# Attention in steps of twenty rows, spread over the four quarters of TensorE

## The chip, the cores and the metric

The kernel runs on one NeuronCore of a Trainium2 chip. The metric is the device time of one execution in microseconds (us). Three runs of the kernel before took 1311.48, 1315.52 and 1314.14 us, with a median of 1314.14 us.

## The reference

The program is three stages in a row. All inputs and the result are 32-bit floats.

```python
# attention: batch 4, 12 heads, 448 rows, head size 64
scores = scale * (q @ k.T)                        # for each head
scores = einsum('bhij,hg->bgij', scores, w_pre)   # premix: the 12 heads are mixed
attn = softmax(scores)                            # along j
attn = einsum('bhij,hg->bgij', attn, w_post)      # postmix: mixed again
x = attn @ v                                      # 1792 rows x 768
x = elu(x @ w_in) @ w_out                         # 768 -> 2048 -> 768
# then each row goes through the one of 8 experts that its gate picks
out[rows of e] = gate * (relu(x @ w1[e]) @ w2[e]) # 768 -> 1024 -> 768
```

The change lies in the first stage alone.

## The kernel before, in words

The first stage (function attention, lines 145 to 424) works through 4 batches of 448 rows in 16 chunks of 110 or 118 rows (CHUNKS, line 26), and through each chunk in 11 or 12 groups of ten rows (a few of nine; GRP, line 27). There are 180 groups in all.

For each chunk, q times k (qk, line 224) is worked out for two heads at a time: the two heads lie in the two halves of 64 partitions, and each takes half of TensorE's rows. q and k are split into a high and a low part in the format fp32r (split_k, split_k_lo, split_q, split_q_lo), and three products (line 233) make up one 32-bit product. The scores leave PSUM by ScalarE and VectorE (qk_out, lines 241 and 243) into a tile st that has rows of the chunk in its partitions and heads beside each other.

The mix over heads needs the heads in the partitions. So for each group one DMA (relayout, line 248), issued on SyncE's queue (SP), moves ten rows of st times 12 heads into 120 partitions of a tile sp. Premix (line 254) is then one 32-bit product of 120x120 weights (a block of w_pre for each of the ten rows) with 448 columns. VectorE takes the maximum (rowmax, line 260), ScalarE the exponential with its sum (expo, line 268), VectorE inverts the sums (norm, lines 277 and 278) and scales the weights of the second mix by them (scale, lines 287 and 289). Postmix (line 298) has the exponentials as its loaded operand and the scaled weights as its moving one, so that it transposes on the way: four 32-bit products with 120 columns. ScalarE copies the result into mt (mt_out, line 305), which has keys in its partitions. Times v (av, line 322) runs for each chunk with two heads in two halves of TensorE's columns, and av_out (lines 329 and 330) sends the result to DRAM.

A 32-bit matmul of the program stands in the trace as two pairs of LDWEIGHTS (weight load) and MATMUL, each of which streams its columns twice; an fp32r one is one pair that streams them once.

The order of the work on every engine is written out by hand: each piece is filed under a slot and an order number (the calls of at, lines 368 to 424), all pieces are sorted by these two numbers, and each engine then does its instructions strictly in that order. Slot x has premix of group x (order 10), postmix of group x-4 (11), then q times k (12) and times v (13) where they fall due. Waits are set by the tiles: a piece waits for the tiles that it reads, and for a free buffer. Around these pieces lies the decoding of some weights of the second stage (lines 128 to 133), 48 halves of it.

The second and third stage (moe1, moe2) begin when the attention is done, with line 523 as the first product.

Of the kernel before, what the change touches and what calls it, by code (L numbers as in the profile page):

```python
# [5 lines left out]
F32 = mybir.dt.float32  # L6
# [13 lines left out]
JC, NJ = 112, 4  # L20
# [5 lines left out]
CHUNKS = [110, 110, 110, 118]  # L26
GRP = [[10] * 11, [10] * 11, [10] * 11, [10] * 10 + [9, 9]]
# [12 lines left out]

def token_orders():


    orders = []
    for n, gs in zip(CHUNKS, GRP):
        G = len(gs)
        starts = [sum(gs[:g]) for g in range(G)]
        order = [0] * n
        for g, T in enumerate(gs):
            for i in range(T):  # L50
                order[g + G * i] = starts[g] + i
        orders.append((order, starts))
    return orders
# [85 lines left out]
for _c in range(NCH):  # L139
    S0.append(S0[-1] + len(GRP[_c % 4]))  # L140
NSLOT = S0[-1]
LAG = 4


def attention(tc, pools, at, q, k, v, kron_pre, kron_post, dec_jobs, xscr):

# [8 lines left out]
    kpre = sb.tile([120, 120], F32, name="kpre")  # L155
    nc.gpsimd.dma_start(kpre, kron_pre)
    nc.vector.tensor_scalar(kpre, kpre, -1.0 / 8.0, None, ALU.mult)
    kpo = sb.tile([120, 120], F32, name="kpo")
    nc.gpsimd.dma_start(kpo, kron_post)
    dec = Decoder(nc, early, 2, 4)  # L160

    (kraw, kr, qraw, qs, qp, st, sp, pre, mxs, pt, sms, rec, kpt, pst, mt, vt, avp,
     draw, dsteps) = ({} for _ in range(19))


    def keys(b, u):
        kr[b, u] = early.tile([128, 2, S], F32R, name="kr", tag="kr", bufs=6)

    def values(b):
        vt[b] = sb.tile([JC, NJ, H, D], F32, name="vt", tag="vt", bufs=2)  # L170
# [6 lines left out]
    def scores(cc):  # L177
        st[cc] = early.tile([118, H, S], F32, name="st", tag=f"st{cc % 2}")

    def load_k(b, u):  # L180
        if b == 0:

            if u == 0:
                scores(0)
                kraw[0] = early.tile([128, H, S], F32, name="k0", tag="st1")
            t = kraw[0][:, u, :]
        else:
            t = early.tile([128, S], F32, name="kraw", tag="kraw", bufs=4)
        nc.sync.dma_start(t, k[b, :, u, :])
        kraw[b, u] = t  # L190

    def split_k(b, u):
        if b:
            keys(b, u)
        if b == 0:
            nc.scalar.activation(kr[b, u][:, 0], kraw[b, u], AF.Copy)
        else:
            nc.vector.tensor_copy(kr[b, u][:, 0], kraw[b, u])

    def split_k_lo(b, u):  # L200
        t = kr[b, u]
        nc.vector.tensor_tensor(t[:, 1], kraw.pop((b, u)), t[:, 0].bitcast(F32), ALU.subtract)

    def load_q(cc, u):
        b, c = divmod(cc, 4)
        n, o = CHUNKS[c], sum(CHUNKS[:c])
        t = early.tile([128, 3 * 118], F32, name="qraw", tag="qraw", bufs=2)
        nc.sync.dma_start(t[:, :3 * n], q[b, :, 6 * o + 3 * n * u:6 * o + 3 * n * (u + 1)])
        qraw[cc, u] = t

    def split_q(cc, u):
        n = CHUNKS[cc % 4]
        t = qs[cc, u] = early.tile([128, 2, 3 * 118], F32R, name="qs", tag="qs", bufs=3)
        nc.scalar.activation(t[:, 0, :3 * n], qraw[cc, u][:, :3 * n], AF.Copy)

    def split_q_lo(cc, u):
        n = CHUNKS[cc % 4]
        t = qs[cc, u]
        nc.vector.tensor_tensor(t[:, 1, :3 * n], qraw.pop((cc, u))[:, :3 * n], t[:, 0, :3 * n].bitcast(F32), ALU.subtract)

    def bank(nm, tag):
        return (ps_qk if tag == "qk" else ps).tile([128, 512], F32, name=nm, tag=tag, bufs=4 if tag == "qk" else 2)

    def qk(cc, u):

        n = CHUNKS[cc % 4]
        tag = {2: "pre", 3: "post"}.get(u, "qk") if cc == 0 else "qk"
        p = qp[cc, u] = [bank("p_qk", tag) for _ in range(2)]
        kk, qq, c = kr[cc // 4, u], qs[cc, u // 3], slice(u % 3 * n, (u % 3 + 1) * n)
        for i, (x, y) in enumerate(((0, 0), (0, 1), (1, 0))):  # L230
            for e in range(2):
                r = slice(64 * e, 64 * e + 64)
                mm(p[e][:n, :S], lhsT=qq[r, x, c], rhs=kk[r, y, :], start=(i == 0), stop=(i == 2))  # L233

    def qk_out(cc, h):
        n = CHUNKS[cc % 4]
        if h == 0 and cc:
            scores(cc)
        src = qp[cc, h // 2][h % 2][:n, :S]
        if h % 2 if cc == 0 else h % 4 == 1:  # L240
            nc.vector.tensor_copy(st[cc][:n, h, :], src)
        else:
            nc.scalar.activation(st[cc][:n, h, :], src, AF.Copy)  # L243

    def relayout(cc, g):
        G, T = len(GRP[cc % 4]), GRP[cc % 4][g]
        t = sb.tile([120, S], F32, name="sp", tag="sp", bufs=4)
        nc.sync.dma_start(t[:12 * T], st[cc][g:g + G * (T - 1) + 1:G])
        sp[cc, g] = t

    def premix(cc, g):
        R = 12 * GRP[cc % 4][g]
        p = bank("p_pre", "pre")
        mm(p[:R, :S], lhsT=kpre[:R, :R], rhs=sp.pop((cc, g))[:R], start=True, stop=True)  # L254
        pre[cc, g] = p
# [1003 lines left out]
```

## Time and profile before

| | |
|---|---|
| median of three runs | 1314.14 us |
| the profiled execution's own time | 1312.17 us |
| its span, first to last instruction | 1310.3 us |
| mean granted clock of TensorE over the span | 0.984 |
| attention, until the first product of the second stage | 479.6 us |
| TensorE busy over the span | 1257.4 us (96%) |
| VectorE / ScalarE / GpSimd busy | 834.2 / 749.9 / 46.0 us |

A busy time is the time in which at least one instruction of the engine was under way. The page gives it for the whole span, and the view of windows for any stretch. The granted clock is the share of TensorE's clock that was let through (1.00 is 2.4 GHz, 0.50 is 1.2 GHz). The chain that ended last is read backwards from the last instruction, at each step to what released it. In the timeline, the time from the start of one entry to the start of the next on the same engine tells what an instruction really costs there, since instructions overlap at their ends.

### The profile page before, as it was taken

How to read it: one execution, taken by the hardware profiler on the slowest of the kernel's cores; microseconds unless marked ns; L12 is line 12 of the kernel's file. 1: busy time of each engine (PE TensorE's matmuls, PEld its weight loads, DVE VectorE, ACT ScalarE, POOL GpSimd, SP SyncE). 2: the span in 40 equal slices, each digit the busy share in tenths (PEclk: the TensorE clock that was granted, in tenths of full speed). 3: DMA queues.
4: the chain of work that ended last, by engine and by line, in shares of the span. 5: the costliest groups of instructions: out<-in, count | busy, mean ns of one | idle time of the engine just before them, and what ended most of it. 6: DMA issues, size and time to landing. Idle time of an engine off the chain costs nothing.

```text
span 1310.3 us, 23113 instructions
## 1 busy us (share of the span) xinstructions
PE 1257.4 (96%) x8622; PEld 1095.4 (84%) x8622; DVE 834.2 (64%) x1815; ACT 749.9 (57%) x1521; POOL 46.0 (4%) x60
## 2 busy tenths in 40 slices
PE   5899999999999989999999999999997999999996
PEld 3577777777677778998899899989996999999996
DVE  4678778778877647887545654664445555666663
ACT  5677767767677555566555555655534444455552
POOL 0000000000000000000000000000001011111110
PEclk8999999999999999999999999999996999999998
DMA  5668667666866448320010011001007647566661
GB/s 153 183 192 243 188 183 234 200 187 200 233 184 180 137 136 331 126 83 2 22 57 8 1 33 46 8 1 43 1 3 250 206 157 231 166 225 222 228 217 56
DMA packets 107340, 181.97 MB, mean 139 GB/s; under 512 B 24755, under 2 KB 75411, under 8 KB 107220
## 3 DMA queue, kind: packets, MB, share of 16 engines
q1 hardware_dynamic: 104468, 168.29, 41.2%
q0 software_dynamic: 2752, 12.12, 2.8%
q8 instruction: 70, 1.15, 0.4%
q14 instruction: 50, 0.41, 0.1%
HBM read 115.88 MB, written 26.95 MB: 109 GB/s over the span
## 4 chain that ended last, share of the span: by engine, by line
PE 90%; DMA 4%; ACT 2%; DVE 2%; issue 1%; SPq 0%; POOL 0%; POOLq 0%; DVEq 0%; ACTq 0%
PE p_h L523 17%; PE acc L585 16%; PE p_h L1031 11%; PE p_pre L254 10%; PE p_post L298 10%; PE p_z L1016 8%; PE p_av L322 6%; PE p_qk L233 5%; PE p_y L1031 3%; DMA sp<-st 2%; PE tp L78 1%; PE p_t L78 1%; DMA xraw<-xscr 1%; DMA raw<-in_w_out_dram 0%; DMA kpre<-in_kron_pre_dram 0%
## 5 line engine op out<-in xcount | busy, mean ns | idle before, releaser
L298 PEld LDWEIGHTS p_post<-kp,pt 120*112 120x112 f32 (+1 forms) x1440 | 175.6, 179 | 74.2 <-issue 50.7
L254 PE MATMUL p_pre<-sp,kpre 120*120 120x448 f32 x360 | 173.2, 564 | 17.2 <-DMA sp<-st 10.8
L298 PE MATMUL p_post<-kp,pt 120*112 120x120 f32 (+1 forms) x1440 | 178.7, 268 | 4.1 <-DVE kp L289 3.7
L260 DVE TENSOR_REDUCE mx<-p_pre 120x1 f32<-120x448 f32 x180 | 111.8, 621 | 75.6 <-PE p_pre L254 74.8
L305 ACT ACTIVATE mt<-p_post 112x480 f32<-112x480 f32 x180 | 103.7, 576 | 77.0 <-PE p_post L298 72.8
L585 PE MATMUL acc<-gh,woh 128*128 128x448 f32 x384 | 142.4, 371 | 0.2 <-ACT gh L482 0.2
L523 PE MATMUL p_h<-xh,wih 128*128 128x448 f32 x384 | 142.3, 371 | 0.0
L585 PE MATMUL acc<-gl,woh 128*128 128x448 f32 x384 | 140.6, 366 | 1.6 <-DVE gl L483 1.6
L523 PE MATMUL p_h<-xh,wil 128*128 128x448 f32 x384 | 140.7, 366 | 0.1
L523 PE MATMUL p_h<-xl,wih 128*128 128x448 f32 x384 | 140.5, 366 | 0.0
L585 PE MATMUL acc<-gh,wol 128*128 128x448 f32 x384 | 140.4, 366 | 0.0
L541 DVE SCALAR_TENSOR_TENSOR th<-rm,th 128x448 f32<-128x448 f32 x64 | 40.0, 625 | 138.2 <-ACT rm L534 138.2
L268 ACT ACTIVATE pt<-p_pre,mx 120x448 f32<-120x448 f32 x180 | 113.3, 630 | 2.3 <-DVE mx L260 2.1
L243 ACT ACTIVATE st<-p_qk 110x448 f32<-110x448 f32 (+1 forms) x141 | 71.7, 542 | 67.0 <-PE p_qk L233 64.2
L1031 PE MATMUL p_h<-xgl,w1h 128*128 128x256 f32 (+1 forms) x384 | 109.7, 286 | 0.2 <-DVE xgl L995 0.2
L1031 PE MATMUL p_h<-xgh,w1h 128*128 128x256 f32 (+1 forms) x384 | 109.9, 286 | 0.0
L1031 PE MATMUL p_h<-xgh,w1l 128*128 128x256 f32 (+1 forms) x384 | 109.6, 285 | 0.0
L100 DVE TENSOR_TENSOR w2l<-w2raw,w2h 128x768 fp32r<-128x768 f32 (+1 forms) x60 | 60.7, 1011 | 51.8 <-ACT w2h L98 51.8
L482 ACT ACTIVATE gh<-g 128x448 fp32r<-128x448 f32 x64 | 37.0, 579 | 93.6 <-DVE g L542 93.6
L322 PEld LDWEIGHTS p_av<-mt,vt 112*64 112x64 f32 x1536 | 73.9, 137 | 17.1 <-ACT st L243 16.4
L531 ACT ACTIVATE rm<-p_h 128x448 f32<-128x448 f32 x64 | 34.7, 542 | 88.2 <-PE p_h L523 88.2
L322 PE MATMUL p_av<-mt,vt 112*64 112x110 f32 (+1 forms) x1536 | 83.5, 262 | 0.8
(159 smaller groups left out, 2547.4 us busy)
## 6 DMA issues: line engine op xcount, KB each, us to landing
sp<-st SPq DMA_DIRECT2D x172, 210.0 KB
w1raw<-in_w_dram SPq DMA_DIRECT2D x64, 384.0 KB
w2raw<-in_w_dram SPq DMA_DIRECT2D x48, 384.0 KB
raw<-in_w_in_dram SPq DMA_DIRECT2D x32, 384.0 KB
raw<-in_w_out_dram SPq DMA_DIRECT2D x32, 384.0 KB
wscr<-wdec SPq DMA_DIRECT2D x32, 192.0 KB
win<-wscr SPq DMA_DIRECT2D x16, 384.0 KB
w2raw<-in_w_dram SPq DMA_DIRECT2D x12, 512.0 KB
```

The source lines that it names most:

```text
L233: mm(p[e][:n, :S], lhsT=qq[r, x, c], rhs=kk[r, y, :], start=(i == 0), stop=(i == 2))
L243: nc.scalar.activation(st[cc][:n, h, :], src, AF.Copy)
L254: mm(p[:R, :S], lhsT=kpre[:R, :R], rhs=sp.pop((cc, g))[:R], start=True, stop=True)
L260: nc.vector.tensor_reduce(mx[:R], pre[cc, g][:R, :S], AX.X, ALU.min)
L268: nc.scalar.activation(e[:R], pre.pop((cc, g))[:R, :S], AF.Exp, bias=mxs.pop((cc, g))[:R], scale=-1.0, accum_out=sms[cc, g // 2][:R, g % 2 ...
L298: mm(p[:JC, j * R:j * R + R], lhsT=e[:R, j * JC:(j + 1) * JC], rhs=kp[:R, :R], start=True, stop=True)
L305: nc.scalar.activation(mt[cc][:, :, :, off:off + T], pst.pop((cc, g)), AF.Copy)
L322: mm(p[64 * e:64 * e + 64, u % 2, :n], lhsT=vt[cc // 4][:, j, 2 * u + e, :], rhs=mt[cc][:, j, 2 * u + e, :n], start=(j == 0), stop=(j == N ...
L523: mm(p[:, :S], lhsT=a[:, c], rhs=m, start=(i == 0), stop=(i == 17))
L585: mm(acc[d][:, :S], lhsT=a[:, c], rhs=m, start=(f == 0 and i == 0), stop=(f == NF - 1 and i == 2))
L1016: mm(zp[p][j, a][:, :384], lhsT=h2[h][:, i, c], rhs=w[:, a * 384:(a + 1) * 384], start=(i == 0 and m == 0), stop=(i == NFE - 1 and m == 2))
L1031: mm(q[:, :N], lhsT=a[:, kk, :], rhs=m[:, kk, :], start=(j == 0), stop=(j == len(seq) - 1))
```

## The change

Chunks have 120, 120, 120 and 88 rows, and each is worked through in units of 20 rows (the last unit of the fourth chunk has 8). There are 92 units: 88 of 20 rows and four of 8.

A unit's rows are dealt to the four quarters of TensorE, 64 rows by 64 columns each. Five rows times 12 heads make 60 partitions, so that a quarter mixes five rows.

- **q times k** takes q and k as they are, in 32 bits, without a split: for two heads four matmuls of 64x64 weights with 448 columns, one in each quarter. The splits of q and k, and their loads into separate tiles, go.
- **The moves** into sp are four DMAs for a unit instead of one for a group: each moves 5 rows times 12 heads (60 partitions of 1792 bytes). They are issued by GpSimd.
- **Premix** is four matmuls of 60x64 weights with 448 columns, one in each quarter, into two PSUM banks.
- **rowmax and expo** run on 128 partitions, two of each for a unit. The inverted sums and the scaled weights of a unit are made by three VectorE instructions.
- **Postmix** is 32 matmuls of 60x64 weights with 60 columns, eight in each quarter, into one PSUM tile of two banks with a single buffer. One ScalarE instruction of 960 elements copies it out.
- **Times v** has the keys in blocks of 128, 128, 128 and 64 (the rest of the last block is zeros) and 120 or 88 columns.
- **The order** is filed by half slots: q times k (order 9) and premix (10) in the first half of a slot, times v (9) and postmix of the unit two before (10) in the second; where q times k falls into a second half it stands there. Three PSUM banks are for premix, two for postmix, two for q times k and one for times v.

```diff
-CHUNKS = [110, 110, 110, 118]
-GRP = [[10] * 11, [10] * 11, [10] * 11, [10] * 10 + [9, 9]]
+CHUNKS = [120, 120, 120, 88]
+UNITS = [[(5, 2)] * 6] * 3 + [[(5, 2)] * 4 + [(4, 1)]]
...
-        for i, (x, y) in enumerate(((0, 0), (0, 1), (1, 0))):
+        for a in range(2):
             for e in range(2):
-                mm(p[e][:n, :S], lhsT=qq[r, x, c], rhs=kk[r, y, :], start=(i == 0), stop=(i == 2))
+                r, c = slice(64 * e, 64 * e + 64), u % 3 * 128 + 64 * a
+                mm(p[64 * a:64 * a + 64, e, :S], lhsT=qq[r, c:c + 64], rhs=kk[r], start=True, stop=True)
...
-        t = sb.tile([120, S], F32, name="sp", tag="sp", bufs=4)
-        nc.sync.dma_start(t[:12 * T], st[cc][g:g + G * (T - 1) + 1:G])
+        t = sp[cc, g] = sb.tile([128, 2, S], F32, name="sp", tag="sp", bufs=3)
+        for r in range(nr):
+            for c in range(2):
+                f, d = first_row(g, r, c, nr), STEP[cc % 4]
+                nc.gpsimd.dma_start(t[64 * r:64 * r + 12 * T, c], st[cc][f:f + d * (T - 1) + 1:d])
...
-        mm(p[:R, :S], lhsT=kpre[:R, :R], rhs=sp.pop((cc, g))[:R], start=True, stop=True)
+        ban = pre[cc, g] = [ps.tile([128, 512], F32, name="p_pre", tag="pre", bufs=3) for _ in range(nr)]
+        for c in range(2):
+            for r in range(nr):
+                x = slice(64 * r, 64 * r + 12 * T)
+                mm(ban[r][64 * c:64 * c + 64, :S], lhsT=kpre[x], rhs=t[x, c, :], start=True, stop=True)
...
-        for j in range(NJ):
-            mm(p[:JC, j * R:j * R + R], lhsT=e[:R, j * JC:(j + 1) * JC], rhs=kp[:R, :R], start=True, stop=True)
+        for j in range(4):
+            for r in range(nr):
+                for s in range(2 * j, 2 * j + 2):
+                    k0 = min(s, 6)
+                    for c in range(2):
+                        x = slice(64 * c, 64 * c + 12 * T)
+                        mm(p[64 * (s % 2):64 * (s % 2) + 64, 2 * c + r, j * 12 * T:(j + 1) * 12 * T],
+                           lhsT=e[x, r, 64 * k0:64 * k0 + 64],
+                           rhs=kp[x, r].rearrange("p (h i) -> p h i", i=5)[:, :, :T], start=True, stop=True)
...
-            at(x - (3 if g or cc else 2), 1, relayout, cc, g)
+            at(x - 2, 1, relayout, cc, g)
             at(x, 10, premix, cc, g)
-            at(x + LAG, 11, postmix, cc, g)
-            at(x + LAG + 1, 28, mt_out, cc, g)
+            at(x + LAG + .5, 10, postmix, cc, g)
+            at(x + LAG + 1, 26, mt_out, cc, g)
```

The number of decoded halves stays 48, and the second and third stage are as they were.

## Rows read from the trace of the kernel before

**Rows 1.** The page: busy time of each engine over the span with its share and instructions, then busy tenths in 40 equal slices of the span, with the granted clock and the share of the DMA engines.

```profile
PE 1257.4 (96%) x8622; PEld 1095.4 (84%) x8622; DVE 834.2 (64%) x1815; ACT 749.9 (57%) x1521; POOL 46.0 (4%) x60
...
PE   5899999999999989999999999999997999999996
...
PEclk8999999999999999999999999999996999999998
```

**Rows 2.** Busy time by window: stretch, its length, then busy time (and instructions) of each engine, granted clock, DMA share, GB/s.

```profile
core 0: us, PE busy (x) PEld busy (x) DVE busy (x) ACT busy (x) POOL busy (x), PEclk, DMA share, GB/s
...
18.64:468.76 450.12, 437.08 (x3738) 327.89 (x3738) 335.09 (x944) 308.61 (x744) 0.00 (x0) 0.99 0.66 195
468.76:479.60 10.84, 6.71 (x43) 5.70 (x44) 8.12 (x18) 8.31 (x17) 0.00 (x0) 0.90 0.67 230
200.00:250.00 50.00, 49.38 (x425) 37.25 (x424) 40.52 (x114) 35.37 (x85) 0.00 (x0) 1.00 0.80 235
479.60:1310.30 830.70, 806.33 (x4806) 756.61 (x4805) 482.69 (x837) 424.57 (x745) 44.47 (x54) 0.98 0.32 107
```

**Rows 3.** The chain that ended last: start, us, what, in the first 20 us, at one chunk boundary, and at the end of attention.

```profile
7.09 6.58 PE p_qk L233 x34
...
14.38 4.12 DMA sp<-st
18.64 1.82 PE p_pre L254 x2
...
105.43 6.13 DMA sp<-st
...
477.80 1.80 PE p_post L298 x8
479.60 7.98 PE p_h L523 x36
```

**Rows 4.** Timeline of TensorE: start, us, what, with counts, at 250 us (chunks of 110 rows) and at 150 us (times v with 118 rows).

```profile
250.42 0.92 PE L254 MATMUL p_pre<-sp,kpre 120*120 120x448 f32 x2
251.18 0.95 PE L298 MATMUL p_post<-kp,pt 108*112 108x108 f32 x8
...
253.60 1.47 PE L233 MATMUL p_qk<-kr,qs 64*110 64x448 f32 x12
255.10 1.73 PE L322 MATMUL p_av<-mt,vt 112*64 112x110 f32 x32
256.75 1.01 PE L254 MATMUL p_pre<-sp,kpre 120*120 120x448 f32 x2
257.60 0.98 PE L298 MATMUL p_post<-kp,pt 120*112 120x120 f32 x8
258.42 0.92 PE L254 MATMUL p_pre<-sp,kpre 120*120 120x448 f32 x2
...
151.96 1.83 PE L322 MATMUL p_av<-mt,vt 112*64 112x118 f32 x32
153.72 1.01 PE L254 MATMUL p_pre<-sp,kpre 120*120 120x448 f32 x2
```

**Rows 5.** Timeline of TensorE at 611 us, in the second stage, where line 649 runs six 32-bit matmuls with 448 columns in four column strips of 32: first within 0.03 us, then until the next group.

```profile
611.53 0.58 PE L649 MATMUL lg<-x,wg 128*32 128x448 f32 x4
...
611.53 1.70 PE L649 MATMUL lg<-x,wg 128*32 128x448 f32 x12
613.16 0.47 PE L585 MATMUL acc<-gh,woh 128*128 128x448 f32 x1
```

**Rows 6.** Timeline of ScalarE at 208 us, and one row at 254 us.

```profile
208.42 0.58 ACT L305 ACTIVATE mt<-p_post 112x480 f32<-112x480 f32 x1
208.88 0.64 ACT L268 ACTIVATE pt<-p_pre,mx 120x448 f32<-120x448 f32 x1
209.39 0.22 ACT L268 ACTIVATION_READ_ACCUMULATOR pt<-p_pre,mx 120x1 f32 x1
209.48 0.63 ACT L129 ACTIVATE dec_p<-dec_p,ebias 128x384 uint32<-128x384 uint32 x1
...
255.10 0.98 ACT L243 ACTIVATE st<-p_qk 110x448 f32<-110x448 f32 x2
```

**Rows 7.** Timeline of VectorE from 208.3 to 212.3 us.

```profile
208.81 0.35 DVE L128 TENSOR_SCALAR dec_p<-raw 128x384 uint32<-128x384 uint32 x1
209.08 0.36 DVE L130 TENSOR_SCALAR dec_m<-raw 128x384 uint32<-128x384 uint32 x1
209.35 0.28 DVE L287 TENSOR_SCALAR kp<-kpo,sm 120x120 f32<-120x120 f32 x1
209.88 0.63 DVE L260 TENSOR_REDUCE mx<-p_pre 120x1 f32<-120x448 f32 x1 [0.25 <-PE p_pre L254]
210.42 0.38 DVE L329 COPY xc<-p_av 128x220 f32<-128x220 f32 x1
210.72 0.49 DVE L219 TENSOR_TENSOR qs<-qraw,qs 128x330 fp32r<-128x330 f32 x1
211.13 0.55 DVE L131 SCALAR_TENSOR_TENSOR dec_m<-raw,dec_m 128x384 f32<-128x384 uint32 x1
211.59 0.16 DVE L277 TENSOR_SCALAR sm<-sm 120x2 f32<-120x2 f32 x1
211.79 0.17 DVE L278 RECIPROCAL sm<-sm 120x2 f32<-120x2 f32 x1
211.99 0.28 DVE L287 TENSOR_SCALAR kp<-kpo,sm 120x120 f32<-120x120 f32 x1
212.19 0.62 DVE L260 TENSOR_REDUCE mx<-p_pre 120x1 f32<-120x448 f32 x1
```

**Rows 8.** Groups of instructions on GpSimd: line, engine, operation, count, busy us and mean ns of one, idle time before.

```profile
L1067 POOL DMA_INDIRECT out_dram<-yrow,put x18 | 24.6, 1368 | 252.4 <-ACT w1h L98 116.2 <-DVE yrow L1058 70.8 <-DVE yrow L1065 64.0
L978 POOL DMA_INDIRECT xg<-x2rows,tok x18 | 18.6, 1033 | 1002.5 <-DMA x2rows<-row 991.4 <-DVE xgl L995 6.2 <-issue 3.7
...
L156 POOL DMA_DIRECT2D kpre<-in_kron_pre_dram x1 | 0.7, 726 | 0.9 <-POOLq L1249 0.9
L159 POOL DMA_DIRECT2D kpo<-in_kron_post_dram x1 | 0.6, 577 | 0.0
```

**Rows 9.** Line 248 by itself: the issue of a move on SP (shortest, median, longest, ns), and who waited for the moves in the whole span (us, times).

```profile
L248 SPq DMA_DIRECT2D sp<-st x180: 760/808/2208, 14.4 to 463.2; - x180
...
  PE p_pre L254: 10.8, 7
```

More of the change, by code (lines that the diff above doesn't have):

```diff
@@ L38, in blocks, with first_row @@
     return [min(128, n - o) for o in range(0, n, 128)]
+def first_row(g, r, c, nr):
+    return 64 * r + 2 * g + c if nr == 2 else 64 * c + 2 * g
 def token_orders():
     orders = []
[L45 to L52, printed above, removed]
+    for us, d in zip(UNITS, STEP):
+        order = [-1] * 128
+        for g, (T, nr) in enumerate(us):
+            for r in range(nr):
+                for c in range(2):
+                    for i in range(T):
+                        order[first_row(g, r, c, nr) + d * i] = 20 * g + (c * nr + r) * T + i
+        orders.append(order)
     return orders
@@ L177, in scores @@
     def scores(cc):
-        st[cc] = early.tile([118, H, S], F32, name="st", tag=f"st{cc % 2}")
+        st[cc] = early.tile([128, H, S], F32, name="st", tag=f"st{cc % 2}")
     def load_k(b, u):
[L181 to L189, printed above, removed]
@@ L190, in load_k @@
-        kraw[b, u] = t
-    def split_k(b, u):
         if b:
             keys(b, u)
[L195 to L202, printed above, removed]
+        elif u == 0:
+            scores(0)
+        nc.sync.dma_start(ks[b, u], k[b, :, u, :])
     def load_q(cc, u):
@@ L345, in attention, with half, take @@
     use = {}
-    def take(slot, **cost):
+    def half(y, order, fn, *args):
+        at(y / 2, order, fn, *args)
+    def take(y, **cost):
         for e, c in cost.items():
-            use[e, slot] = use.get((e, slot), 0) + c
-        return slot
+            use[e, y] = use.get((e, y), 0) + c
+        return y
     def room(lo, hi, **cost):
-        return take(min(range(lo, max(lo, hi) + 1), key=lambda x: max(use.get((e, x), 0) + c for e, c in cost.items())), **cost)
-    def block(cc, u):
+        return take(min(range(lo, max(lo, hi) + 1), key=lambda y: max(use.get((e, y), 0) + c for e, c in cost.items())), **cost)
@@ L368, in attention @@
     for cc in range(NCH):
-        z, G = S0[cc], len(GRP[cc % 4])
+        z = S0[cc]
         for u in range(6):
-            x = block(cc, u)
-            at(x, 12, qk, cc, u)
-            at(x, 33, qk_out, cc, 2 * u)
-            at(x if cc else x + 1, 33 if cc else 29, qk_out, cc, 2 * u + 1)
-            if u % 2 and cc:
-                take(x, act=162 - 300, dve=54 - 300)
-        for g in range(G):
+            y = when(cc, u)
+            half(y, 9, qk, cc, u)
+            half(y + 1, 5, qk_out, cc, u)
+            take(y + 1, act=54 if u % 2 else 90, dve=62 if u % 2 else 0)
@@ L390, in attention @@
-            take(x + 3, dve=20)
-            at(x + LAG, 11, postmix, cc, g)
-            at(x + LAG + 1, 28, mt_out, cc, g)
-            take(x + LAG + 1, act=57)
+            at(x + LAG, 20, scale, cc, g)
+            for r in range(nr):
+                at(x, 22, rowmax, cc, g, r)
+                at(x + 1, 24, expo, cc, g, r)
+            at(x + LAG + .5, 10, postmix, cc, g)
+            at(x + LAG + 1, 26, mt_out, cc, g)
+            take(2 * x, dve=185, act=200)
+            take(2 * x + 1, act=60)
@@ L414, in attention @@
-            at(f - 6 if cc else (-20, -18)[u], 3, load_q, cc, u)
-            at(x, 40, split_q, cc, u)
-            at(room(x + 1, f - 1, dve=50) if cc else x, 41, split_q_lo, cc, u)
+            half(when(cc, 3 * u) - 8 if cc else (-40, -36)[u], 3, load_q, cc, u)
     N = 2 * len(dec_jobs)
```

289 lines of the change are left out of this document (129 added, 160 removed).

## The prediction, made before the changed kernel was built

> **What bounds the kernel now.** I read the page first. TensorE is busy 96% of the span and no other engine over 64% [rows 1], so the question is what the change does to TensorE's time, and who is next when that falls. The granted clock stands at 9 (full) in nearly every slice, so no stage is waiting for clock.
>
> The windows come next, since the change touches one stage only. From the first premix at 18.64 us to the last at 468.76 us TensorE is busy 437.1 of 450.1 us, VectorE 335.1 and ScalarE 308.6; 13 us of the stretch are waits. The stage ends at 479.6 us, and the 830.7 us behind it are untouched [rows 2]. The chain of waits confirms it: short DMA pieces at the start (4.12 us of a move before the first premix) and at a chunk boundary (6.13 us), else TensorE's own products [rows 3]. So attention is bound by TensorE's columns, with 18.6 us of lead-in and 10.8 us of tail.
>
> What each product costs is read from the timeline, from start to start [rows 4]. Premix: 251.18 - 250.42 = 0.76 us. Postmix: 258.42 - 257.60 = 0.82 us. Q times k for four heads (12 pairs of weight load and matmul): 255.10 - 253.60 = 1.50 us. Times v for four heads (32 pairs): 256.75 - 255.10 = 1.65 us with 110 columns, 153.72 - 151.96 = 1.76 us with 118. Sum: 180 groups x (0.76 + 0.82) + 48 x (1.50 + 1.65) = 284.4 + 151.2 = 435.6 us, which is the stretch's 437.1 us of busy time. The other 44.0 us of the 479.6 are lead-in, tail and waits.
>
> **TensorE's part of the change.** The question is whether four quarters work at once. The trace has no product in quarters, but both halves of the answer. Two column strips: in times v, 32 pairs with 110 columns streamed twice are 32 x 220 / 2.4 GHz = 2.93 us one after another and take 1.65. Four strips: line 649 starts four matmuls within 0.03 us, and six of them, 6 x 1792 columns / 2.4 GHz = 4.48 us by themselves, are over in 613.16 - 611.53 = 1.63 us [rows 5]. Two row halves: q times k starts 12 matmuls of 448 columns, 2.24 us by themselves, and takes 1.50 [rows 4]. I take it that strips and halves go together.
>
> - Premix: a unit's four matmuls with 448 columns, side by side, last as long as one: 0.76 us for 20 rows where two groups took 1.52. 92 x 0.76 = 69.9 us against 136.8.
> - Q times k: four 32-bit matmuls with 448 columns side by side, the same 0.76 us for two heads, where half of 1.50 stood. 96 x 0.76 = 73.0 us against 72.0. The exact product costs four streams instead of three, and the quarters pay for it.
> - Times v: from 110 to 118 columns 32 pairs grow by 0.11 us, or 0.0138 us a column. With 120 columns 1.79 us (36 times), with 88 1.35 us (12 times): 80.6 us against 79.2.
> - Postmix: a unit has 32 matmuls of 60 columns, 64 pairs, in four quarters. By the slope of times v, 32 pairs of 60 columns in two strips would take 1.65 - 50 x 0.0138 = 0.96 us; 64 pairs in four quarters the same. 92 x 0.96 = 88.3 us against 147.6. From below, columns alone: 64 x 120 / 2.4 / 4 = 0.80 us. From above, a pair costs what one costs in times v however short it is: 64 x 1.65 / 32 = 3.30 us. I take 0.96, because the pair's time did follow its columns between the two rows.
>
> Sum: 69.9 + 73.0 + 80.6 + 88.3 = 311.8 us, 123.8 us less than 435.6.
>
> **Who is next.** Per unit of 20 rows TensorE has 0.76 + 0.79 + 0.96 = 2.51 us in a slot without times v and 4.30 us in one with it, and 48 such pieces over 92 units make this every other slot. ScalarE [rows 6]: two exponentials with their sums 2 x (209.48 - 208.88) = 1.20; copying out 960 elements at most 2 x 0.46 (208.88 - 208.42) = 0.92; scores 3 x 0.98 + 3 x 0.49 for a chunk of 5.75 units = 0.77; decoding 0.63 x 48/92 = 0.33. Together 3.22 us. VectorE [rows 7]: two maxima 2 x 0.54 = 1.08; three small ones 212.19 - 211.59 = 0.60; scores 0.54 x 48/92 = 0.28; xc 0.30 x 48/92 = 0.16; five steps of decoding 0.27 + 0.27 + 3 x 0.46 = 1.92 x 48/92 = 1.00. Together 3.12 us. The splits of q and k and half of the scalings are gone from both.
>
> So in every other slot TensorE would be through in 2.5 us and the two need 3.2. Postmix has a single buffer and premix three banks for two a unit, so TensorE can't run far ahead: I charge the difference in full, 46 x 0.7 = 32 us. From below it is nothing, if the buffers let the slots even out.
>
> **The moves.** 88 units x 4 + 4 x 2 = 360 DMAs go from SP to GpSimd's queue. GpSimd has nothing else to do before the gathers of the third stage, but for the two first loads and four clearings of a tile; SP has 180 issues of 0.81 us fewer [rows 9], and gains nothing, since TensorE waited only 10.8 us for moves in all [rows 9]. What such an issue costs on GpSimd the trace shows for plain loads of 120 partitions, 0.73 and 0.58 us, and for indirect ones, 1.03 and 1.37 us [rows 8]. I take the mean of the plain ones, 0.65: 360 x 0.65 = 234 us, 2.6 us a unit, hidden behind units of some 3.9 us. From below 0.58 (208 us), from above 1.37 (493 us, rival 2). The landing (4.12 and 6.13 us [rows 3]) has two slots, 7 us and more. At a chunk boundary, four issues and a landing, 2.6 + 6.1 = 8.7 us, come up to what lies between the last scores and the premix that wants them; I leave the waits of before standing for it, with 15 x 2 = 30 us as the upper end. DMA traffic is the same bytes in less time: 0.66 x 450 us = 297 us in some 360 is a share of 0.83, and a stretch with 0.80 kept TensorE at 49.4 of 50 us [rows 2].
>
> Lead-in: four issues in a row, and slower 32-bit products at a low clock, before the first premix: +4 us. Tail: LAG is shorter and slots are longer: +1 us.
>
> **Forecast.** Stage: 479.6 - 123.8 + 32 + 5 = 392.8 us, 86.8 less. From the profiled execution's 1312.17 us that is 1225 us; the median of the runs is 2 us above that execution, which I leave out. Its own range: with nothing charged for the other engines 1193, with as much again 1257.
>
> **Rivals.**
>
> 1. *The other engines' chain takes over everywhere.* Premix, maximum, exponential, scaling, postmix and copy hang together over few buffers; if each slot lasts as long as one with times v, 4.3 us: 18.6 + 4 + 91 x 4.3 + 12 = 426 us, 1259. For it: ScalarE and VectorE would be at 3.2 of 3.9 us. Against: now VectorE is busy 335 of 450 us and TensorE still lost only 13.
> 2. *GpSimd becomes the bound.* At the price of an indirect issue, 1.03 us, 371 us of issues and 36 us of ends make 407 us, 1240; at 1.37, 493 + 36 = 529 us, 1361, slower than before. It decides from 443 / 360 = 1.23 us an issue. For it: no move between partitions issued there is in the trace, and VectorE's work may hold it up. Against: the plain loads at 0.58 and 0.73. The Trainium skill (SBUF — State Buffer, "SBUF: two separate sides") says that GpSimd can't write descriptors while VectorE runs an operation that takes both ports, as a 32-bit copy between SBUF tiles does; no row of before has the two side by side. If every issue waited out one such step of 0.35 us [rows 7], 360 x 1.00 = 360 us, it would just reach the stage's length.
> 3. *Short pairs cost as much as long ones.* At 52 ns a pair (1.65 / 32 [rows 4]), postmix is 3.30 us a unit: 92 x 2.34 = 215 us more TensorE time, which swallows the 32 us: 479.6 - 123.8 + 215 + 5 = 576 us, 1408, slower. It decides from 2.25 us a unit, 35 ns a pair. The Trainium skill (TensorE: Matmul & The Clock Gate, "Back-to-back issue gap") puts a stream of load-and-matmul pairs with 128 columns at about 81 ns each, by which 64 pairs would be 5.2 us and the kernel far slower; here pairs of 118 columns in two strips take 1.76 / 32 = 55 ns, so the measurement decides against that figure.
>
> **Chances.** Forecast 0.48; rival 1 0.18; rival 2 0.21, of it 0.12 on the faster side; rival 3 0.09; sums of these that come out even 0.04. Differences under 0.3%, some 4 us, can't be told from none here. Faster 0.48 + 0.18 + 0.12 = 0.78, same 0.04, slower 0.09 + 0.09 = 0.18. The range goes from 1182 (the forecast's lower end with shorter waits) to 1295, where GpSimd at 1.18 us an issue still lies within it; the slow halves of rivals 2 and 3 stay outside.
>
> **What would show it.** Right: the first product of line 523's stage starts near 393 us; premix and q times k take 0.76 us for four matmuls, postmix about 1 us for 64 pairs; TensorE's busy share in attention falls from 97% to some 80 to 90%, with its waits on ScalarE's copies and exponentials. Wrong: a postmix over 2 us (rival 3), GpSimd busy without a break or premix waiting for moves in most units (rival 2), four matmuls of premix that take 1.5 us (then quarters work as halves).

## The result, and the profile after

The changed kernel takes 1271.5 us (median of four runs, 1271.0 to 1276.4) against 1312.8 in the same session: a ratio of 0.970, 95% interval 0.966 to 0.974. The gain is 41 us. The forecast was 1225 us and 87 us of gain: the direction came true, and the time lies in the range of 1182 to 1295, but less than half of the gain came. The profiled execution took 1271.0 us.

The page of the changed kernel: busy time by engine, the granted clock in 40 slices, and the DMA queues. In all rows PE is TensorE, PEld its weight loads, DVE is VectorE, ACT ScalarE, POOL GpSimd and SP SyncE.

```profile
span 1269.2 us, 32519 instructions
...
PE 1162.9 (92%) x13494; PEld 983.2 (77%) x13494; DVE 783.1 (62%) x1645; ACT 727.3 (57%) x1350; POOL 257.4 (20%) x424
...
PEclk8998999998999799999999999999988999999998
...
q0 software_dynamic: 31552, 50.82, 15.2%
q8 instruction: 108, 1.77, 0.6%
```

The first product of the second stage stands at 434.4 us where it stood at 479.6 [rows 2]. The stage gave 45 us, and the rest of the kernel is 4 us longer.

The window from the first premix to the last, which answers to the first window of [rows 2]: length, busy time (and instructions) of each engine, granted clock, DMA share, GB/s.

```profile
22.83:421.63 398.80, 340.12 (x8469) 220.19 (x8470) 288.22 (x781) 286.97 (x579) 205.38 (x355) 0.96 0.81 214
```

The lead-in of 22.8 us (forecast 22.6) and the tail of 12.8 (forecast 11.8) came out as worked out. The loss lies in this window: it was to last 358 us (450.1 - 123.8 + 32), 313 of them TensorE's and 45 of waits, and lasts 399, with TensorE busy for 340 and idle for 59.

TensorE's groups of products take about what was forecast, but for premix. Its timeline in a quiet stretch (start, length, group, idle time before it), to be set against [rows 4]:

```profile
53.19 1.16 PE L279 MATMUL p_post<-kp,pt 60*64 60x60 f32 x64 [0.66 <-ACT mt L289]
54.46 0.98 PE L218 MATMUL p_qk<-ks,qs 64*64 64x448 f32 x8
55.26 0.93 PE L245 MATMUL p_pre<-sp,kpre 60*64 60x448 f32 x8
56.74 1.16 PE L279 MATMUL p_post<-kp,pt 60*64 60x60 f32 x64 [0.55 <-DVE kp L266]
57.69 0.59 PE L218 MATMUL p_qk<-ks,qs 64*64 64x448 f32 x4
```

From start to start, 57.69 - 56.74 = 0.95 us for the 64 pairs of a postmix (forecast 0.96, 15 ns a pair) and 55.26 - 54.46 = 0.80 for a q times k (0.76). Four quarters do work at once. Premix, forecast at 0.76, depends on what follows it. Both places are at full clock:

```profile
63.23 1.02 PE L245 MATMUL p_pre<-sp,kpre 60*64 60x448 f32 x8
63.98 1.20 PE L279 MATMUL p_post<-kp,pt 60*64 60x60 f32 x64
...
82.80 1.02 PE L245 MATMUL p_pre<-sp,kpre 60*64 60x448 f32 x8
83.75 1.86 PE L314 MATMUL p_av<-mt,vt 128*64 128x120 f32 x32
85.54 1.16 PE L279 MATMUL p_post<-kp,pt 60*64 60x60 f32 x64
```

It takes 63.98 - 63.23 = 0.75 us ahead of a postmix and 83.75 - 82.80 = 0.95 ahead of a times v, which itself takes 85.54 - 83.75 = 1.79, as forecast. Over all places of the window at full clock and without a wait, the medians are 0.76 (25 places) and 0.95 (31 places).

TensorE's waits in the window: waiting group, what it waited for, us in total, times, longest.

```profile
PE p_post L279 <- issue: 16.0, 13, 5.1
PE p_qk L218 <- DVE st L226: 15.6, 16, 2.1
PE p_av L314 <- DVE xc L321: 9.5, 4, 2.8
PE p_pre L245 <- DMA sp<-st: 9.5, 1, 9.5
PE p_qk L218 <- ACT st L228: 6.2, 5, 3.0
PE p_post L279 <- ACT mt L289: 3.6, 7, 0.7
PE p_pre L245 <- issue: 2.0, 3, 1.6
...
PE p_av L314 <- issue: 1.6, 3, 1.1
```

The 9.5 us for a move are the lead-in, reckoned to the first premix. What is left falls in two: 38 us for VectorE and ScalarE, where the forecast had 45 of waits in all, and 20 us named issue, in which TensorE waited for nothing that the profile shows. The kernel before had none of that kind in the stretch of [rows 2], where its 13 us of waits were for moves and for ScalarE. The longest, in TensorE's timeline:

```profile
99.33 0.92 PE L279 MATMUL p_post<-kp,pt 60*64 60x60 f32 x47
105.36 0.79 PE L279 MATMUL p_post<-kp,pt 60*64 60x60 f32 x17 [5.11 <-issue]
105.84 1.06 PE L218 MATMUL p_qk<-ks,qs 64*64 64x448 f32 x4
```

It cuts a postmix in two: all its operands are there, and after 47 of the 64 products nothing follows for 5.11 us. The DMA queues from 98 to 106 us (packets, MB, share of 16 engines):

```profile
q1 hardware_dynamic: 619, 1.33, 66.5%
q0 software_dynamic: 504, 0.72, 38.3%
q8 instruction: 1, 0.02, 0.9%
```

One packet of the instruction queue lies in these 8 us, with the engines full (the shares sum to 1.06). Its start, 102.81, and end, 103.94, stand in the trace; TensorE goes on 1.4 us behind the end. I counted TensorE's instructions in the trace in order (products, loads and its sequencer's waits). All 19 issue waits over 0.2 us in the window, 20.2 us together, stand at the same place modulo 256, and each ends 1.2 to 1.6 us behind such a packet of 16 KB. I read them as waits for instructions. The window has 67 of these packets for 17160 instructions, 256 each; the stretch of [rows 2] had 30, in more time.

The Trainium skill (Runtime: NRT & Kernel Launch, "Instruction fetch mechanics") says that an engine's instructions come in blocks of 16 KiB, 256 instructions each, over a DMA queue of its own, and that crossing from one block to the next is mostly hidden. The block agrees with the 1.77 MB in 108 packets; in this stage the crossing is not hidden, with 20 us of waits.

The pause is paid twice. From 105.40 to 108.00 the granted clock is 0.50, the lower level of 1.2 GHz, and the q times k there takes 1.50 us instead of 0.76:

```profile
105.40:108.00 2.60, 2.60 (x29) 1.43 (x33) 0.00 (x0) 1.46 (x2) 0.00 (x0) 0.50 1.06 236
```

### The profile page after: what moved, and what is told of

It is laid out like the page before. It is cut to its first block, busy times and chain, and to the rows that moved or that the text cites. A ratio compares the mean times of both kernels' runs of the same rounds, so it can differ in the third digit from the quotient of the medians.

```text
span 1269.2 us, 32519 instructions
## 1 busy us (share of the span) xinstructions
PE 1162.9 (92%) x13494; PEld 983.2 (77%) x13494; DVE 783.1 (62%) x1645; ACT 727.3 (57%) x1350; POOL 257.4 (20%) x424
## 3 DMA queue, kind: packets, MB, share of 16 engines
q0 software_dynamic: 31552, 50.82, 15.2%
q8 instruction: 108, 1.77, 0.6%
## 4 chain that ended last, share of the span: by engine, by line
PE 81%; DVE 6%; DMA 6%; issue 3%; ACT 3%; POOL 1%; POOLq 0%; SPq 0%; ACTq 0%; DVEq 0%
PE p_h L495 18%; PE acc L557 17%; PE p_h L1003 11%; PE p_z L988 8%; PE p_post L279 5%; PE p_av L314 5%; PE p_pre L245 5%; PE p_qk L218 5%; DMA sp<-st 3%; PE p_y L1003 3%; DVE mx L250 2%; DVE st L226 1%; PE tp L86 1%; DMA raw<-in_w_out_dram 1%; PE p_t L86 1%
## 5 line engine op out<-in xcount | busy, mean ns | idle before, releaser
L236 POOL DMA_DIRECT2D sp<-st x360 | 207.9, 594 | 195.9 <-PE p_pre L245 102.7
L250 DVE TENSOR_REDUCE mx<-p_pre 128x1 f32<-128x448 f32 x180 | 104.2, 619 | 101.6 <-PE p_pre L245 101.1
L279 PEld LDWEIGHTS p_post<-kp,pt 60*64 60x64 f32 (+1 forms) x5760 | 103.2, 141 | 65.4 <-ACT mt L289 32.8
L279 PE MATMUL p_post<-kp,pt 60*64 60x60 f32 (+1 forms) x5760 | 114.2, 227 | 29.5 <-issue 16.0
L289 ACT ACTIVATE mt<-p_post 128x960 f32<-128x960 f32 (+1 forms) x92 | 102.0, 1108 | 54.5 <-PE p_post L279 54.1
L256 ACT ACTIVATE pt<-p_pre,mx 128x448 f32<-128x448 f32 x180 | 112.7, 633 | 25.0 <-DVE mx L250 24.3
L218 PE MATMUL p_qk<-ks,qs 64*64 64x448 f32 x744 | 98.5, 576 | 26.9 <-DVE st L226 15.6
L314 PEld LDWEIGHTS p_av<-mt,vt 128*64 128x64 f32 x1536 | 77.3, 141 | 44.2 <-issue 21.8
L245 PE MATMUL p_pre<-sp,kpre 60*64 60x448 f32 x720 | 100.5, 555 | 11.5 <-DMA sp<-st 9.5
L314 PE MATMUL p_av<-mt,vt 128*64 128x120 f32 (+1 forms) x1536 | 87.8, 269 | 11.1 <-DVE xc L321 9.5
```

The source lines that it names most:

```text
L218: mm(p[64 * a:64 * a + 64, e, :S], lhsT=qq[r, c:c + 64], rhs=kk[r], start=True, stop=True)
L236: nc.gpsimd.dma_start(t[64 * r:64 * r + 12 * T, c], st[cc][f:f + d * (T - 1) + 1:d])
L245: mm(ban[r][64 * c:64 * c + 64, :S], lhsT=kpre[x], rhs=t[x, c, :], start=True, stop=True)
L250: nc.vector.tensor_reduce(mxs[cc, g][:, r:r + 1], pre[cc, g][r][:, :S], AX.X, ALU.min)
L256: nc.scalar.activation(pt[cc, g][:, r], pre[cc, g][r][:, :S], AF.Exp, bias=mxs[cc, g][:, r:r + 1], scale=-1.0, accum_out=sms[cc, g][:, r:r ...
L279: mm(p[64 * (s % 2):64 * (s % 2) + 64, 2 * c + r, j * 12 * T:(j + 1) * 12 * T], lhsT=e[x, r, 64 * k0:64 * k0 + 64], rhs=kp[x, r].rearrange ...
```

## The experiments

Theory at the start: the missing gain went into DMA, as moves that land late and as instructions that come late behind other traffic (0.81 of the engines' time, up to 0.93 in stretches). Rival: the chain of VectorE and ScalarE over single buffers. "Stage" below is the time of the second stage's first product, from one profiled execution; the runs of one kernel spread by up to 15 us (three_scores_early: 1253 to 1269), so that a stage difference under 10 us is not read by itself. Where no interval stands, there was one run.

**Decoding: transfers and steps apart.** 19 of the 24 weight tiles are decoded in the second stage instead (no_decoding), or their transfers stay in attention (transfers_only), or their engine steps (steps_only).

```diff
+        if n not in (0, 1, 2, 16, 17):
+            continue
...
-                             xscr, wscr, oscr, x2rows, R, before)
+                             xscr, wscr[:3], oscr[:2], x2rows, R, before)
```

> 19 of the 24 weight tiles that attention decodes on the side are decoded in the second stage instead, so that four fifths of those transfers (some 22 of 92 MB) and of those steps (some 58 us of VectorE, 19 us of ScalarE) leave attention. Only the end of the stage (the first p_h product, 434.4 us in the changed kernel) is compared, since the second stage is longer by the work moved into it. Both theories let it fall. Theory DMA (the missing 42 us are moves that land late and TensorE's waits named issue, both from full DMA engines): 395 to 405 us, no wait named issue over 1 us, moves land in under 4 us in the median. Rival (the chain of VectorE and ScalarE over single buffers): also below 415, but the waits named issue stay.

> As in no_decoding, but the transfers of the 19 tiles stay in attention (loads as before, the raw words are written to a scratch that nobody reads), only VectorE's and ScalarE's steps are gone. Theory DMA: the stage still ends at 422 to 434 us, with the long issue waits and the landing of 5 us as they were. Rival (engines' chain): 395 to 410 us.

> As in no_decoding, but the steps of VectorE and ScalarE for the 19 tiles stay in attention, on one tile loaded once, whose results nobody reads; the transfers are gone. Theory DMA: the stage ends at 400 to 410 us, waits named issue under 1 us each. Rival (engines' chain): 422 to 434 us, as with the transfers.

| | stage | issue waits | waits for VectorE, ScalarE | clock | DMA share |
|---|---|---|---|---|---|
| changed kernel | 434.4 | 20.4 | 38 | 0.96 | 0.81 |
| transfers_only | 431.9 | 24.1 | 36 | 0.97 | 0.83 |
| steps_only | 423.9 | 15.2 | 35 | 0.96 | 0.61 |
| no_decoding | 401.6 | 12.2 | 30 | 0.99 | 0.65 |

(Columns from the waits and the window between the first and last premix of each.) Transfers alone keep the stage long, as the DMA theory had it. Steps alone should then have given 400 to 410 and gave 424: a miss for it. So is no_decoding, where no wait named issue was to be over 1 us and the longest has 3.2. Either half brings back most of the 33 us, so one does not add to the other; both theories are partly right. The moves land in 5 us in the median in the changed kernel; the traces of the other three don't tell it. The whole takes 1337.6, 1324.6 and 1305.1 us (transfers_only, steps_only, no_decoding), since the second stage has more to decode.

**Fewer instructions by 128 output rows (halves).** Three of four column blocks of postmix, and q times k, in row halves.

```diff
+            mm(p[:, e, :S], lhsT=qq[r, c:c + 128], rhs=kk[r], start=True, stop=True)
...
+                if j < 3:
+                    for c in range(2):
+                        x = slice(64 * c, 64 * c + 12 * T)
+                        mm(p[:, 2 * c + r, j * 12 * T:(j + 1) * 12 * T], lhsT=e[x, r, 128 * j:128 * j + 128],
+                           rhs=kp[x, r].rearrange("p (h i) -> p h i", i=5)[:, :, :T], start=True, stop=True)
```

> The changed kernel with q times k, and three of the four column blocks of postmix, written in row halves with 128 output rows instead of quarters with 64: same columns for the array, same result, but 40 pairs instead of 64 for a postmix and 4 instead of 8 products for a q times k, some 6200 pairs in attention instead of 8800. If TensorE's issue waits come once for each block of instructions, there are 29% fewer of them, and the stage ends 5 to 8 us sooner (426 to 430 us). If they have to do with time or with DMA alone, or only the engines' chain counts, the stage stays at 434 within 2 us. If a load of 128 columns costs a row half more than two of 64 in quarters, postmix rises from 0.95 us and the stage gets longer.

1322.2 us, ratio 1.007 (1.004 to 1.010), stage 486. The last expected case came. TensorE's timeline:

```profile
201.32 1.55 PE L276 MATMUL p_post<-kp,pt 60*128 60x60 f32 x24
202.80 0.46 PE L284 MATMUL p_post<-kp,pt 60*64 60x60 f32 x16
203.19 1.02 PE L217 MATMUL p_qk<-ks,qs 64*128 64x448 f32 x4
204.14 0.61 PE L244 MATMUL p_pre<-sp,kpre 60*64 60x448 f32 x4
```

24 pairs in halves take 202.80 - 201.32 = 1.48 us; the 48 in quarters that they replace take 48 x 0.95 / 64 = 0.71. But no wait named issue is left among TensorE's waits, at a DMA share of 0.71: with 6015 + 6016 products and loads in 450 us a block of 256 has 9.6 us, where the changed kernel gives it 398.8 x 256 / 16939 = 6.0.

**Landing of the moves (three_scores, three_scores_early).**

```diff
-        st[cc] = early.tile([128, H, S], F32, name="st", tag=f"st{cc % 2}")
+        st[cc] = early.tile([128, H, S], F32, name="st", tag=f"st{cc % 3}")
...
-        lo, hi = max(S0[cc - 1] - 2, 0), S0[cc] - 2
+        lo, hi = max(S0[cc - 1] - 3, 0), S0[cc] - 3
```

The second of the two cuts is in three_scores_early alone.

> The changed kernel with three score buffers instead of two, nothing else. In its trace TensorE's q times k waits 22 us in all for copies into st, and behind the longest (3.0 us) ScalarE's copy waits for the moves of the chunk before the last to land, since they still read the buffer. Theory landing (moves of 5 us in the median, up to 10, show where a buffer is written again right behind them): waits of q times k for st fall from 22 to some 10 us and the stage ends 8 to 15 us sooner, at 420 to 426 us. Rival (those waits come from VectorE and ScalarE being behind with their own work): no change within 3 us.

> As three_scores, and every chunk's q times k a slot earlier, so that the moves of a new chunk's first unit have three slots to land instead of two. Theory landing: another 5 to 10 us off, the stage ends at 410 to 420 us. Rival (engines' chain): as the changed kernel, 434 within 3 us.

The third buffer alone: 1272.2 us, ratio 0.968 (0.965 to 0.970), stage 434.2. Waits for ScalarE fell from 10.6 to 4.9 us and those named issue rose to 26.5: the rival's number, and a sign of what takes the place of a removed wait. With q times k a slot earlier as well: 1262.1 us, 0.958 (0.952 to 0.964), stage 428.7 (in the longest of its four runs), between both expectations. By the medians, landing at chunk boundaries is worth some 10 us of the 42 that the stage is longer than forecast.

**The issuing engine (moves_on_sp).** `nc.gpsimd.dma_start` in relayout becomes `nc.sync.dma_start`.

> The changed kernel with its 360 moves issued by SyncE's queue again, as in the kernel before. If an issue costs SyncE the 0.81 us of before, the moves alone take 290 us there, behind some 180 other issues of attention that wait for their own tiles: theory landing: TensorE's waits for moves rise and the stage ends at 450 us or later. Rival (the issuing engine doesn't matter): 434 within 5 us.

Stage 525.3 us, the whole 1361: slower than the kernel before. Two rows: the issues on SyncE (ns min, median, max), and TensorE's largest group of waits.

```profile
L236 SPq DMA_DIRECT2D sp<-st x360: 642/730/1408, 13.8 to 499.8; - x180
```

```profile
PE p_qk L218 <- ACT st L228: 46.9, 15, 6.6
```

ScalarE's copies into st waited in their turn 38 us for the moves of an earlier chunk, which stood late in SyncE's queue and still read the buffer. Moving the issues to GpSimd is worth 91 us of the stage.

**Less decoding (four_later).** `oscr` has four tiles instead of eight.

> The changed kernel with 8 of the 48 half tiles decoded in the second stage instead of in attention (four tiles fewer of the second weight matrix): a sixth of the decoding's transfers and steps leaves attention. Where both the transfers and the steps hold attention up (removing four fifths of both gave 33 us), a sixth is worth 5 to 8 us: stage 427 to 430 us. In the second stage 8 more half tiles are decoded beside TensorE, which is 99% busy there; if they hide, the whole is 5 to 8 us faster (some 1264), if not, each costs up to the 1.75 us that the 38 cost there, and the whole is some 8 us slower.

1261.9 us, 0.960 (0.956 to 0.964), stage 423.3: a sixth of the decoding out of attention gives 10 us, somewhat more than expected, and the second stage hides nearly all of it. early_four and early_two below join it to the earlier q times k.

**Times v spread out, copies moved (av_spread, scores_first).**

```diff
-        y = 2 * (S0[cc + 1] + (2 if cc >= NCH - 2 else 3 + 2 * a)) + 1
+        y = 2 * (S0[cc + 1] + (2 if cc >= NCH - 2 else 3 + 2 * a - (cc % 4 == 2))) + 1
```
```diff
-            half(y + 1, 5, qk_out, cc, u)
+            half(y, 21, qk_out, cc, u)
```

> The changed kernel with times v of the chunk before each short one (88 tokens, five units) a slot earlier, so that no two times v stand in neighbouring slots on their single PSUM buffer. In the changed kernel TensorE waits 2.3 to 2.8 us there for the copy into xc, at 137.5, 240.0 and 342.3 us, and the granted clock stands below 0.9 in the windows right behind. Theory (a pause costs its length and the low clock behind it): the three waits go, 7.8 us, and the clock drops with them, 2 to 3 us each: stage 12 to 17 us sooner, 417 to 422 us. Rival (the pause alone, or it moves to the next wait): 0 to 8 us sooner.

> The changed kernel with the copies of q times k out of PSUM half a slot earlier in the queues of VectorE and ScalarE, ahead of the two maxima and the exponentials instead of behind them. Theory (q times k waits 22 us for st because the copies stand behind two maxima that wait for premix): these waits fall to under 10 us and the stage ends 8 to 15 us sooner, 420 to 427 us. Rival (the engines are simply full): the wait moves to the maxima and exponentials, and the stage stays at 434 within 4 us or gets longer.

av_spread: 1270.4 us, 0.969 (0.965 to 0.972), stage 436.6, no sooner. The three waits for xc went, but times v now waits at three other places, nearly as long (7.8 us before):

```profile
PE p_av L314 <- ACT pt L256: 7.2, 3, 2.8
```

Waits for VectorE fell from 27 to 11 us, those for ScalarE rose from 11 to 17 and issue waits from 20 to 32. So the pauses moved, and the granted clock stayed at 0.96: that a pause also costs the low clock behind it was not put to the test by this run.

scores_first: 1373.4 us, 1.047 (1.043 to 1.050), stage 540. Its chain of waits, one unit (start, us, what):

```profile
207.01 0.80 PE p_qk L218 x8
...
208.65 1.34 ACT pt L256 x4
209.98 1.02 ACT mt L289
...
211.05 1.16 PE p_post L279 x64
212.21 0.80 PE p_qk L218 x8
```

ScalarE's copy of q times k now stands before the exponentials and the copy of postmix; the next postmix waits for that copy, and the next q times k stands behind that postmix: a loop of 5 to 6 us a unit. The two versions that joined all edits so far (all_four, all_two) held scores_first and were slower with it, 1364.1 us, 1.038 (1.035 to 1.042), and 1377.9 us, 1.050 (1.047 to 1.053); nothing about adding up can be read from them.

> Three score buffers with q times k a slot earlier, av_spread, scores_first, and four tiles of the second weight matrix left to the second stage, together. If the parts add up: stage 434 - 6 - 14 - 10 - 11 = 393 us, which is the forecast's 392.8, and the whole some 1235 us. If they are several faces of one bound (the engines' chain), not below 415 us and 1255 us.

> As all_four, with two more tiles (four more half tiles) left to the second stage. If the second stage hides them as it hid the first eight, another 4 to 6 us off the whole; if it is full, the whole is 0 to 5 us longer than all_four.

**VectorE's copy alone, and parts joined (dve_first, early_four, early_two, early_no_decoding).** In dve_first only VectorE's half of the copies goes ahead of the maxima.

```diff
...
+            if cc == 0 or u % 2:
+                half(y + (cc == 0), 5 if cc == 0 else 21, qk_out, cc, u, True)
```

> The changed kernel with VectorE's half of the copies of q times k ahead of the two maxima of its slot, ScalarE's copies where they were. In the run that moved both, ScalarE's copies stood in front of exponentials and copies of postmix for which TensorE had to wait before it came to q times k: a loop of 5.5 us a unit. VectorE's copy has no such loop: the maxima behind it wait for premix, which TensorE issues right behind q times k. Theory (order in the queue): the 15.6 us that q times k waits for VectorE's copies fall under 5 and the stage ends 5 to 12 us sooner, 422 to 430 us. Rival (the engines are full, waits only move): 434 within 3 us. If VectorE's copy closes a loop as well, it is longer by tens of us.

> Three score buffers with q times k a slot earlier, and four tiles of the second weight matrix left to the second stage. Alone the two gave 9 to 10 us of the whole each. If they add up: stage 417, the whole 1252 to 1254 us. If they remove the same waits: 1260 to 1262 us.

> As early_four with two more tiles left to the second stage. If the second stage hides these four half tiles too: another 4 to 6 us off, 1247 us; if it is full there, 1252 to 1260 us.

> No_decoding (four fifths of the decoding done in the second stage) with three score buffers and q times k a slot earlier. Only the end of the stage is compared; it was 401.6 us without the earlier q times k. If what is left are landings at chunk boundaries: 392 to 396 us. If it is TensorE's clock, its issue waits (12 us left there) and the engines' order: 399 to 403 us.

dve_first: 1268.5 us, 0.966 (0.962 to 0.970), stage 433.2: the waits of q times k for VectorE's copies went, and the stage is the rival's. VectorE's waits fell from 27 to 10 us, ScalarE's rose from 11 to 18 and issue waits from 20 to 25. early_four: 1264.0 us, 0.963 (0.960 to 0.965), stage 430.1: no more than each alone, as if they removed the same waits. early_two: 1275.2 us, 0.971 (0.968 to 0.974), above both expectations, with the stage at 428.3: the second stage does not hide the next four half tiles. early_no_decoding: stage 412.2, above the 401.6 without the earlier q times k and outside both expectations; not explained.

**More instructions (more_products), three orders (orders).** In three_scores, av_spread and dve_first waits for the engines fell, and waits named issue grew. So instructions, not the engines, might set the pace. more_products adds instructions and no columns; orders joins three_scores_early, dve_first and av_spread.

```diff
+        for o in (0, 224):
...
-                mm(p[64 * a:64 * a + 64, e, :S], lhsT=qq[r, c:c + 64], rhs=kk[r], start=True, stop=True)
+                    mm(p[64 * a:64 * a + 64, e, o:o + 224], lhsT=qq[r, c:c + 64], rhs=kk[r, o:o + 224], start=True, stop=True)
...
-                mm(ban[r][64 * c:64 * c + 64, :S], lhsT=kpre[x], rhs=t[x, c, :], start=True, stop=True)
+                    mm(ban[r][64 * c:64 * c + 64, o:o + 224], lhsT=kpre[x], rhs=t[x, c, o:o + 224], start=True, stop=True)
```

> The changed kernel with every product of q times k and of premix split in two of 224 columns, same result and same columns: 744 products more, of four instructions each (TensorE's record shows two pairs of load and matmul for one 32-bit product), so some 3000 more of 17000 between the first and the last premix, 12 more blocks of 256. Theory (the supply of instructions paces TensorE, about 5 to 6 us a block of 256): waits named issue rise from 21 us to 40 or more, and the stage ends 20 to 60 us later, 455 to 495 us. Rival (issue waits are accidents of DMA traffic, the engines' chain paces): what the extra loads cost on TensorE itself, at most 0.1 us a product group, and no more: 434 to 450 us with issue waits of 21 to 25 us.

> Three score buffers with q times k a slot earlier, VectorE's copies first, and times v spread out, together. If the waits for VectorE and ScalarE were the loss, and add up: from 38 us to some 15, and the stage ends at 408 to 415 us, the whole near 1250 us. If instructions pace TensorE: the waits named issue take their place (30 us or more) and the stage ends at 422 to 432 us, the whole at 1258 to 1268 us.

Both came nearer to what the supply of instructions would have; only the whole time of orders lies 3 us above its range. more_products: 1300.3 us, stage 460.3, 120 packets of the instruction queue instead of 108, DMA share 0.75. Its window and waits:

```profile
22.98:448.30 425.32, 348.78 (x9903) 285.84 (x9904) 287.84 (x781) 288.21 (x579) 206.43 (x355) 0.94 0.75 202
```

```profile
PE p_post L281 <- issue: 30.4, 19, 3.7
PE p_qk L219 <- DVE st L227: 12.3, 15, 1.9
...
PE p_qk L219 <- issue: 6.2, 5, 2.5
PE p_av L316 <- issue: 6.0, 4, 3.3
PE p_pre L247 <- issue: 3.6, 2, 2.7
```

Issue waits 46 us instead of 20, and the window 26.5 us longer, of which TensorE's busy time has 8.7; all 29 over 0.2 us stand again at the one place modulo 256. A block has 425.3 x 256 / 19807 = 5.5 us.

orders: 1271.2 us, 0.968 (0.964 to 0.972), stage 432.2. VectorE's waits are down to 5.6 us, and the sum of all waits is almost where it was:

```profile
PE p_post L280 <- issue: 27.5, 18, 4.6
...
PE p_qk L218 <- issue: 4.9, 3, 3.5
PE p_post L280 <- ACT mt L290: 4.7, 11, 0.7
...
PE p_av L315 <- issue: 2.4, 3, 1.1
```

34.8 us of issue waits (all 24 over 0.2 us at the one place), 20 of the engines: 55 against 58.

## Why the prediction was right and wrong

**TensorE's part** was right in its mechanism: quarters work at once, 64 short pairs take 0.95 us, q times k 0.76 to 0.80 and times v 1.79. Premix was too cheap, as said below. Rival 3 (short pairs cost 52 ns) is out: 15 ns. The figure of 81 ns for a pair with 128 columns in the Trainium skill (TensorE: Matmul & The Clock Gate, "Back-to-back issue gap") is far from these short pairs in quarters too.

**The issues on GpSimd** were right: 360 issues in 207.9 us (234 forecast), 583 ns in the median and 832 at most, with VectorE busy 72% of the window.

```profile
L236 POOL DMA_DIRECT2D sp<-st x360 | 207.9, 594 | 195.9 <-PE p_pre L245 102.7 <-issue 41.4 <-PE p_post L279 14.4
```

Rival 2 is out; no issue came near the 1.23 us from which it decides. What the prediction missed is that SyncE's part matters (it "gains nothing"): with the moves on its queue the stage is 91 us longer (moves_on_sp).

**The waits of the engines**, 32 + 13 = 45 us forecast, came out at 38.

**The step that failed** is the sum for the stage, 479.6 - 123.8 + 32 + 5. By it the window between the first and the last premix lasts 358 us; it lasted 399. Against 7 us less of engine waits stand three things, some 47 us together:

- *Waits for instructions, 20 us*, for which the sum has no term. "DMA traffic is the same bytes in less time ... a share of 0.83" was taken as harmless because a stretch with 0.80 kept TensorE at 49.4 of 50 us. The share was right (0.81). But that stretch of [rows 2] had 425 + 424 instructions of TensorE in 50 us, 3.3 blocks of 256, and the changed kernel has some 2100 (16939 x 50 / 398.8), 8.3 blocks.
- *The clock, some 12 us*, for which it has no term either. By the granted clock, 0.96 over 399 us, some 16 us are lost, against 4 before (an estimate). Besides the low clock of the lead-in, which reaches 5.6 us into it, the window has seven stretches at 0.50, the lower level: two begin in a wait for instructions (5.1 and 2.7 us), with 10 us of low clock, five in or behind waits of 2.0 to 3.0 us for VectorE or ScalarE, with 17 us. So pauses of either kind stand ahead of it.
- *TensorE's saving, some 15 us short.* Its busy time fell by 437 - 340 = 97 us, not by 123.8, and by 109 when the clock's 12 us are taken out. Counted from start to start of the groups, idle time left out and time at 0.50 taken half, premix fell by 57 us instead of 67, postmix by 58 instead of 59, q times k rose by 4 instead of 1 and times v by 2 instead of 1. The term that was too large is premix's saving: 0.76 us was charged in every unit, and it takes 0.95 where times v follows, 45 times in the window. Why this change costs 0.2 us no run here shows.

The trace of before showed such a price of changing from one product to another: its postmix took 0.82 us ahead of a premix and 0.91 ahead of a q times k (medians of 115 and 43 places). The prediction didn't see it because its sum, 435.6 us, agreed with the stretch's 437.1. That was in part luck: it counts 48 pieces of q times k and of times v, of which the stretch holds 45 each, 9.5 us less.

**Rival 1** came nearest in time (4.38 us a unit against its 4.3, 1259 us), but not by its mechanism: with the engines' waits lowered from 38 us to 20, 28 and 27 (orders, dve_first, av_spread) the time moved by no more than 3 us, within the intervals, since issue waits rose in their place. Its loop is real where the order lets it close, as scores_first showed. Shown: instructions added without columns lengthen the stage by 26 us (one run), and where TensorE takes its instructions more slowly the issue waits go or nearly go (none in halves, 2 us in moves_on_sp, 3 in scores_first). Not shown: that a kernel with fewer instructions at the same speed would reach 393 us; no such version was found, as halves cost more on TensorE than it saved.

Three versions beat both kernels: four_later, three_scores_early and early_four, 8 to 10 us below the changed kernel, with intervals below its own.

## What to carry to other kernels

When a change trades long products for many short ones, count TensorE's instructions per us beside its columns, and put 256 of them against the time in which the trace lets a 16 KB packet of the instruction queue through. Where several waits are near the same size, taking one away shows the next; an edit that adds to one cause (here more instructions, same columns) tells more. Price a group of products together with the group that follows it, and look at how many pieces a stretch holds before its busy time is taken to confirm a sum.

## What the runs showed of the hardware

- In the changed kernel TensorE waited up to 5.1 us in the middle of a group for instructions, only at one place of every 256, and went on 1.2 to 1.6 us behind a 16 KB packet of the instruction queue; the stage took one such packet in 6.0 us on average, one in 5.5 with more_products.
- Premix in quarters took 0.76 us ahead of a postmix in quarters and 0.95 us ahead of a times v, whose weight loads have 128 rows (medians at full clock).
- 60-column pairs with weight loads of 128 columns took 62 ns each in row halves, 15 ns with 64 columns in quarters.
- A DMA issue of 60 rows took 0.58 us on GpSimd and 0.73 on SyncE in the median.
